# Moving the operands of the matrix products to other offsets within 128 bytes of on-chip memory

## The chip, the core and the metric

The kernel runs on one core of one Trainium2 chip. The metric is the device time of one execution in microseconds. The core has a matrix engine (TensorE; PE in the profile, its loads of stationary operands are PEld), three elementwise engines (VectorE = DVE, ScalarE = ACT, GpSimd = POOL), a queue engine (SyncE = SP) and 16 DMA engines. On-chip memory has 128 partitions; a tile has the same byte address in each of them, and this document speaks of that address: its remainder by 128 is called the offset here, offsets 0 to 63 are the low half and 64 to 127 the high half.

A product on PE has two operands in on-chip memory: a stationary block of 128 columns, which PEld loads into the array first, and moving rows (here 256, 260 or 512 columns), which stream through it. PEld loads the block of the next product while the moving rows of the present one stream.

## The reference

```
# q, k, v: 4 batches, 8 heads, 768 positions, 64 wide; n_sink = 4, window = 128
scores = q @ k^T / 8; kept where key < n_sink or 0 <= query - key < window, else -1e9
a = exp(scores - max); a = a / (sum(a) + 1e-9)
x = (a @ v), heads side by side: 3072 tokens x 512
h = x @ w_in            # 512 x 2048
g = h - tanh(h)
out = g @ w_out         # 2048 x 512, float32
```

## The kernel before

The 3072 tokens are cut into 12 chunks of 256, the 2048 hidden columns into 8 groups of 256. A step is one chunk with one group, 96 steps in all. Attention of a chunk is done for 4 pairs of heads (48 units); raw units work in float32, from the fourth chunk on queries and keys are split into a rounded high part and a rest (type float32r) and multiplied in pieces.

The first half of a step is 24 products of 256 columns (`mm1`, L793): a block of w_in is stationary, x is moving. x lies split in tiles xh (high) and xl (low). The blocks of w_in of the first three chunks (576 products) stand in resident tiles named w; for the later nine chunks (1728 products) they are streamed from DRAM into a ring of seven places, four in a tile named ring, three in one named spare, which hold 990 and 738 products.

The second half multiplies g with w_out. g lies split in tiles ghbuf and glbuf, whose blocks are stationary; w_out (tile w, or tile edge for derived sums of blocks) is moving. Steps of the first five chunks, and the last step, do it as 12 products of 512 columns (`mm2`, L863): 41 steps, 492 products. The other 55 steps use a scheme of seven block products, 21 products of 256 columns each (`mm7`, L897): 1155 products. The split scores (`scores`, L514) are 8 products of 260 columns for each of 36 units: 288, with a tile q as stationary and a tile ks as moving operand. Values times probabilities (L662), raw scores (L507) and transposes (L599, L640) are float32.

The order on each engine is written out by a planner (`Work.order`) from hand-given durations and due times; it knows nothing of addresses. Addresses come from the pools: tiles are laid one behind another in the order in which their pools and tags are opened, each start rounded up to 32 bytes. So a tile that is made longer moves all that lies behind it.

Of the kernel before, what the change touches and what calls it, by code (L numbers as in the profile page):

```python
# [9 lines left out]
F32 = mybir.dt.float32  # L10
F32R = mybir.dt.float32r
I32 = mybir.dt.int32
# [6 lines left out]
P = 128  # L19
# [7 lines left out]
KW = WIN + TS  # L27
KPACK = P + NT * TS
CH = 2 * P
# [10 lines left out]
@with_exitstack  # L40
def kernel(
    ctx: ExitStack,
    tc: tile.TileContext,
    qd: bass.AP,
    kp: bass.AP,
    vp: bass.AP,
    vs: bass.AP,
    nsw: bass.AP,
    w_in: bass.AP,
    w_out: bass.AP,  # L50
    xd: bass.AP,
    out: bass.AP,
):
    nc = tc.nc

    cpool = ctx.enter_context(tc.tile_pool(name="cpool", bufs=1))
    ident = cpool.tile([P, P], F32, tag="ident", name="ident")
    nswi = cpool.tile([P, 4], I32, tag="nswi", name="nswi")

    pts = cpool.tile([P, NPAIR, 2, 4, P], F32, tag="pt", name="pt")  # L60
    early = []
    for m in range(2):
        first = pts[:, m].rearrange("p h a b -> p (h a b)")
        early.append((first[:, :KW], first[:, KW : KW + 2 * CH].rearrange("p (h s) -> p h s", h=2)))
    et = mybir.EngineType
    with tc.manual_schedule(engines={et.PE, et.SP, et.DVE, et.Activation, et.Pool}):

        scr = pts[:, 2, 0]
        nc.sync.dma_start(nswi, nsw.partition_broadcast(P))
        for m in range(2):  # L70
            k, q = early[m]
            nc.sync.dma_start(k, kp[0, m, :, :KW])
            _load_pair(nc, q, qd[0, 2 * m : 2 * m + 2, :, :CH], True)
            if m == 0:
                make_identity(nc, ident)
                nc.gpsimd.iota(scr[:, 0, :].bitcast(I32), pattern=[[-1, P]], base=0, channel_multiplier=1)
                nc.gpsimd.iota(scr[:, 1, :].bitcast(I32), pattern=[[1, P]], base=0, channel_multiplier=0)
        masks = _masks(nc, cpool, nswi, scr)
        _, (nlo, nhi, wlo, whi) = nc.values_load_multi_w_load_instructions(
            nsw[0:1, 0:4], skip_runtime_bounds_check_because="every value takes one of the two branches"  # L80
        )
        bad = nhi | whi | ((nlo + 3) >> 3) | ((wlo - 1) >> 7)


        WARM = 3
        with tc.tile_pool(name="warm", bufs=1, space=PSUM) as wp:
            warm = wp.tile([P, P], F32, tag="warm", name="warm")
            for _ in range(WARM):
                nc.tensor.matmul(warm, lhsT=ident, rhs=ident, start=True, stop=True)

    with tc.If(bad == 0) as cmp:
        _banded(tc, qd, kp, vp, vs, masks, w_in, w_out, ident, pts, early, out)
    with cmp.Else():
        _general(tc, qd, kp, vp, nswi, w_in, w_out, ident, xd, out)


def _load_pair(nc, q, src, zeros):


    for h in range(2):  # L100
        r, z = slice(64 * h, 64 * h + 64), slice(64 * (1 - h), 64 * (1 - h) + 64)
        if zeros:
            nc.gpsimd.memset(q[z, h, :], 0.0)
        nc.sync.dma_start(q[r, h, :], src[h, r])
# [128 lines left out]
def _banded(tc, qd, kp, vp, vs, masks, w_in, w_out, ident, pts, early, out):  # L233
    nc = tc.nc
    et = mybir.EngineType
    with ExitStack() as ctx:

        def pool(name, bufs, **kw):
            return ctx.enter_context(tc.tile_pool(name=name, bufs=bufs, **kw))

        cpool, wpool, wmpool = pool("cpool", 1), pool("wpool", 1), pool("wmpool", 1)
        qpool, kpool, vpool, hpool = pool("qpool", 1), pool("kpool", 1), pool("vpool", 3), pool("hpool", 1)
        pp, sm = pool("pp", 2), pool("sm", 4)
        xpool, gpool = pool("xpool", 2), pool("gpool", 1)
# [8 lines left out]
        flat = wide.rearrange("p a b c -> p (a b c)")  # L253
        gbuf = gpool.tile([P, 8, P], F32, tag="gbuf", name="gbuf")
        ghbuf = gpool.tile([P, 2, 7, P], F32R, tag="ghbuf", name="ghbuf")
        glbuf = gpool.tile([P, 8, P], F32R, tag="glbuf", name="glbuf")
        wscr = dpool.tile([NG, P, 2 * WG], F32, tag="wscr", name="wscr")
        bscr = dpool.tile([NG, P, 5, DM // 2], F32, tag="bscr", name="bscr")
        kscr = dpool.tile([2, P, 2, DM // 2], F32, tag="kscr", name="kscr")
# [31 lines left out]
        qt, kt, vt, wraw = {}, {}, {}, {}  # L291
# [12 lines left out]
        def unit(u):  # L304
            cc, p = divmod(u, NPAIR)
            return (cc, p, *chunks[cc])
# [5 lines left out]
        def wtag(k, g):  # L312
            return f"w{k}_{g if k else g % NSLOT}"
# [5 lines left out]
        def load_qk(u):  # L319
            cc, p, b, c = unit(u)  # L320

            def lend():
                if u == 3:
                    if u not in place_of:
                        place_of[u] = gpool.tile([P, 3 * WG // 2], F32, tag="spare", name="qk3")
                    return place_of[u]
                if lent[u] not in place_of:
                    k, g = lent[u]
                    place_of[lent[u]] = wpool.tile([P, 2 * WG], F32, tag=wtag(k, g), name=f"qk{u}")
                return place_of[lent[u]][:, u % 2 * WG : u % 2 * WG + WG]  # L330

            def keys():
                if u in lent or u == 3:
                    kt[u] = lend()[:, 2 * CH : 2 * CH + KW]
                else:
                    kt[u] = kpool.tile([P, KW], F32, tag="kraw", name=f"kraw{u}")
                (nc.gpsimd if LQ and not raw(u) else nc.sync).dma_start(kt[u], kp[b, p, :, 2 * c * TS : 2 * c * TS + KW])

            def queries():
                if not raw(u):  # L340
                    qt[u] = qpool.tile([P, 2, CH], F32, tag="qraw", name=f"qraw{u}")
                src = qd[b, 2 * p : 2 * p + 2, :, c * CH : (c + 1) * CH]
                if raw(u):
                    _load_pair(nc, qt[u], src, False)
                else:
                    (nc.gpsimd if LQ else nc.sync).dma_start(qt[u], src.rearrange("h d s -> d h s"))  # L346

            def zeros():
                if u in lent or u == 3:
                    qt[u] = lend()[:, : 2 * CH].rearrange("p (h s) -> p h s", h=2)  # L350
                else:
                    qt[u] = qpool.tile([P, 2, CH], F32, tag="qraw", name=f"qraw{u}")
                nc.gpsimd.memset(qt[u], 0.0)

            t = due_unit(u) - 8000
            if raw(u):
                work.add("POOL", 460, t - ZL, zeros, (), [slots(u)[1]])
            e = "POOL" if LQ and not raw(u) else "SP"
            work.add(e, 600, t, keys, (), [slots(u)[0], "seq k"], lands=800 if raw(u) else 1000)
            work.add(e, 800, t, queries, (), [slots(u)[1], "seq q"], lands=600 if raw(u) else 1000)  # L360

# [49 lines left out]

        zt = cpool.tile([P, 2, NPAIR, 4, 2, NSK], F32R, tag="z", name="z")

        zr = cpool.tile([P, 2, CH], F32R, tag="zr", name="zr")

        mask, above, below, after, rest = masks

# [44 lines left out]
        qh, ql, ks, pr, st, xps, xh, xl, sps, tps = ({} for _ in range(10))  # L462

        def split(u):

            def k_high(h):
                if h == 0:
                    t = hpool.tile([P, NPAIR * CH], F32R, tag="ha", name=f"ks{u}")  # L470
                    ks[u] = t[:, : 2 * KW].rearrange("p (h k) -> p h k", h=2)
                r = slice(64 * h, 64 * h + 64)
                nc.scalar.copy(ks[u][r, h, :], kt[u][r, :])  # L473

            def k_low(h):
                k, t = ks[u], kt[u]
                r, o = slice(64 * h, 64 * h + 64), slice(64 * (1 - h), 64 * (1 - h) + 64)
                (nc.gpsimd if KP else nc.vector).tensor_tensor(k[o, h, :], t[r, :], k[r, h, :].bitcast(F32), op=ALU.subtract)  # L478

            def q_high():  # L480
                t = hpool.tile([P, 2, 2, CH], F32R, tag="hb", name=f"q{u}")
                qh[u], ql[u] = t[:, 0], t[:, 1]
                nc.scalar.copy(qh[u], qt[u])

            def q_low():
                (nc.gpsimd if QP else nc.vector).tensor_tensor(ql[u], qt[u], qh[u].bitcast(F32), op=ALU.subtract)  # L486

            t = due_unit(u) - 5000
            k, q = ([s] for s in slots(u))
            old = [("x", 2)] + [("xu", 2, i) for i in range(NPAIR)] if u == 3 * NPAIR else []  # L490
            work.add("ACT", 525, t, q_high, q, ["qh"] + old)
            work.add("POOL" if QP else "DVE", 1360 if QP else 705, t, q_low, q + ["qh"], ["ql"], port=True)
            for h in range(2):
                work.add("ACT", 425, t, lambda h=h: k_high(h), k, [("ks", h)] + old)
                work.add("POOL" if KP else "DVE", 1050 if KP else 590, t, lambda h=h: k_low(h), k, [("ks", h)], port=True)
# [853 lines left out]
```

## Time and profile before

| | before |
|---|---|
| median of 3 runs | 687.06 us (685.87 to 687.35) |
| the profiled execution: its time | 685.92 us |
| its span, first to last instruction | 684.2 us |
| granted TensorE clock, mean of the span | 0.997 |
| PE busy | 665.0 us, 97% |
| DVE / ACT / POOL busy | 78% / 60% / 30% |

The profiled execution is 1.14 us below the median. Its time is 1.7 us longer than its span. PE's record of a product lasts from its start to the modelled end of the pipeline, so records overlap: what a product costs in a stream is the distance from its start to the start of the next.

### The profile page before, as it was taken

Reading aid. Unit: us, or ns where it says so; the run is one execution under the profiler, and the core shown is the slowest. Engines: PE = TensorE matmul, PEld = TensorE weight load, DVE = VectorE, ACT = ScalarE, POOL = GpSimd, SP = SyncE. Lnnn points to the kernel's source line nnn. Section 1 sums busy time; section 2 is a strip of 40 time slices with the busy share of each in tenths; the row PEclk is TensorE's granted clock in tenths of the full one; section 3 lists DMA queues with packets and bytes.
Section 4 is the critical chain, followed back from the end, with each engine's and each line's share of the span. In section 5 each row is a group of like instructions: output and inputs, shape, how many; then the busy total and the mean of one; then the engine's idle time right before and its main releaser. Section 6 shows DMA issues by size and latency. Waiting matters only on the chain.

```text
span 684.2 us, 14570 instructions
## 1 busy us (share of the span) xinstructions
PE 665.0 (97%) x5099; PEld 613.8 (90%) x5099; DVE 531.4 (78%) x1365; ACT 412.7 (60%) x1056; POOL 204.7 (30%) x363
## 2 busy tenths in 40 slices
PE   6899999999999999999999999999999999999995
PEld 4677899989888898899999999999999999999995
DVE  6999988965998875577698797888888888755654
ACT  5986444435998876466676576676676567533331
POOL 5444000002985532334432323422223222300100
PEclk9999999999999999999999999999999999999998
DMA  6878896785999577799977767766667766656861
GB/s 178 269 252 273 283 308 242 285 280 155 199 209 289 182 228 222 216 290 284 265 223 215 230 176 233 231 209 207 215 216 231 245 192 168 206 160 196 261 187 35
DMA packets 79342, 152.96 MB, mean 224 GB/s; under 512 B 9565, under 2 KB 25565, under 8 KB 79261
## 3 DMA queue, kind: packets, MB, share of 16 engines
q1 hardware_dynamic: 65884, 121.65, 56.7%
q0 software_dynamic: 13376, 30.30, 16.4%
q8 instruction: 42, 0.69, 0.4%
q14 instruction: 40, 0.32, 0.1%
HBM read 131.47 MB, written 20.45 MB: 222 GB/s over the span
## 4 chain that ended last, share of the span: by engine, by line
PE 83%; POOL 4%; DVE 4%; ACT 4%; DMA 2%; issue 2%; SPq 0%; POOLq 0%; DVEq 0%; ACTq 0%
PE h L793 35%; PE s L897 11%; PE o L897 8%; PE o L863 8%; PE x L662 3%; PE s L863 3%; PE t L599 2%; PE t L662 2%; PE t L514 2%; PE t L863 2%; PE x L514 2%; PE x L863 2%; POOL edge L995 1%; PE s L514 1%; DMA v<-vp 1%
## 5 line engine op out<-in xcount | busy, mean ns | idle before, releaser
L793 PE MATMUL h<-xh,ring 128*128 128x256 f32 x660 | 133.5, 282 | 0.0
L812 ACT ACTIVATE gbuf<-h 128x512 f32<-128x512 f32 x96 | 57.2, 596 | 86.7 <-PE h L793 58.9
L793 PEld LDWEIGHTS h<-xh,ring 128*128 128x128 f32 x660 | 107.8, 188 | 0.4 <-PE t L662 0.2
L793 PE MATMUL h<-xh,spare 128*128 128x256 f32 x492 | 100.0, 283 | 0.0
L346 POOL DMA_DIRECT2D qraw<-qd x36 | 29.6, 821 | 222.7 <-DVE q L486 198.4
L793 PE MATMUL h<-xl,ring 128*128 128x256 f32 x330 | 92.2, 279 | 0.0
L539 ACT ACTIVATE p<-p,st 128x132 f32<-128x132 f32 x168 | 66.9, 400 | 27.8 <-DVE st L531 26.6
L831 ACT CAST ghbuf<-gbuf 128x896 fp32r<-128x896 f32 x55 | 51.8, 942 | 49.0 <-DVE gbuf L828 48.6
L793 PEld LDWEIGHTS h<-xh,spare 128*128 128x128 f32 x492 | 81.0, 190 | 0.3
L834 DVE TENSOR_TENSOR glbuf<-gbuf,ghbuf 128x896 fp32r<-128x896 f32 x55 | 60.3, 1097 | 20.1 <-ACT ghbuf L831 15.1
L793 PE MATMUL h<-xh,w 128*128 128x256 f32 x384 | 74.0, 282 | 0.0
L793 PE MATMUL h<-xl,spare 128*128 128x256 f32 x246 | 69.4, 282 | 0.0
L793 PEld LDWEIGHTS h<-xl,ring 128*128 128x128 f32 x330 | 62.1, 188 | 0.3
L793 PEld LDWEIGHTS h<-xh,w 128*128 128x128 f32 x384 | 61.1, 188 | 1.3 <-PE x L662 0.2
L565 ACT ACTIVATE p<-p,st 128x132 f32<-128x132 f32 x168 | 54.2, 394 | 3.5 <-DVE st L560 3.1
L815 DVE TENSOR_TENSOR gbuf<-h,gbuf 128x512 f32<-128x512 f32 x55 | 37.8, 687 | 21.9 <-ACT gbuf L812 21.3
L793 PE MATMUL h<-xl,w 128*128 128x256 f32 x192 | 53.8, 280 | 0.0
L619 POOL TENSOR_TENSOR pt<-pt,after 128x512 f32<-128x512 f32 x32 | 44.1, 1379 | 25.5 <-ACT pt L616 24.1
L863 PE MATMUL o<-w,ghbuf 128*128 128x512 f32 x192 | 50.8, 399 | 0.1
L793 PEld LDWEIGHTS h<-xl,spare 128*128 128x128 f32 x246 | 46.7, 190 | 0.3
L815 DVE TENSOR_TENSOR h<-h,gbuf 128x512 f32<-128x512 f32 x41 | 28.5, 695 | 19.1 <-ACT gbuf L812 19.0
L478 DVE TENSOR_TENSOR ks<-kraw,ks 64x392 fp32r<-64x392 f32 x72 | 40.5, 562 | 3.5 <-ACT ks L473 1.4
(174 smaller groups left out, 1693.2 us busy)
## 6 DMA issues: line engine op xcount, KB each, us to landing
ring<-wscr SPq DMA_DIRECT2D x165, 256.0 KB, 4.3
spare<-wscr SPq DMA_DIRECT2D x123, 256.0 KB, 4.5
qraw<-qd POOLq DMA_DIRECT2D x36, 256.0 KB, 5.2
wraw<-w_in SPq DMA_DIRECT2D x16, 512.0 KB, 6.4
wraw<-w_out SPq DMA_DIRECT2D x16, 512.0 KB, 6.9
wscr<-w SPq DMA_DIRECT2D x16, 512.0 KB, 6.0
kraw<-kp POOLq DMA_DIRECT2D x36, 196.0 KB, 4.5
v<-vp POOLq DMA_DIRECT2D x18, 256.0 KB, 3.3
```

The lines of the kernel that those rows point to most:

```text
L478: (nc.gpsimd if KP else nc.vector).tensor_tensor(k[o, h, :], t[r, :], k[r, h, :].bitcast(F32), op=ALU.subtract)
L514: nc.tensor.matmul(ps[h][:, :WIN], lhsT=q[:, h, t * P : (t + 1) * P], rhs=rhs, start=i == 0, stop=i == 1,)
L539: nc.scalar.activation(e, e, AF.Exp, bias=st[u][:, j : j + 1], scale=-1.0, accum_out=st[u][:, 4 + j : 5 + j],)
L565: nc.scalar.activation(pr[u][:, j, :], pr[u][:, j, :], AF.Copy, scale=s[:, 8 + j : 9 + j])
L619: nc.gpsimd.tensor_tensor(w[:, :, 0, :], w[:, :, 0, :], after.unsqueeze(1).to_broadcast([P, 4, P]), op=ALU.mult)
L793: nc.tensor.matmul(hps[n][:, f, :], lhsT=w, rhs=x, start=r == 0, stop=r == 11)
L812: nc.scalar.activation(g0, h(), AF.Tanh)
L815: nc.vector.tensor_tensor(g0 if strassen(n) else h(), h(), g0, op=ALU.subtract)
L831: nc.scalar.copy(ghbuf[:, n % 2], gbuf[:, 1:, :])
L834: nc.vector.tensor_tensor(glbuf[:, :7, :], gbuf[:, 1:, :], ghbuf[:, n % 2].bitcast(F32), op=ALU.subtract)
L863: nc.tensor.matmul(sums_of(n, cc, t), lhsT=a[:, f, t * P : (t + 1) * P], rhs=wt[1, g][:, (0, 1, 0)[i], f, :], start=first and not low and ...
L897: nc.tensor.matmul(acc, lhsT=a[:, b, :], rhs=factor(g, m, part % 2), start=g == 0 and part == 0 and m in (4, 1, 2, 7), stop=closes(n) and ...
```

## The change

Five tiles are made longer or start later, and the views used by the program are cut out of them, so no instruction is added, taken away or reordered: on all five engines the program has the same rows in the same order. What is different are the addresses of operands.

```
-    nswi = cpool.tile([P, 4], I32, tag="nswi", name="nswi")
+    nswi = cpool.tile([P, 12], I32, tag="nswi", name="nswi")[:, :4]
...
-        glbuf = gpool.tile([P, 8, P], F32R, tag="glbuf", name="glbuf")
+        glbuf = gpool.tile([P, 8 * P + 16], F32R, tag="glbuf", name="glbuf")[:, : 8 * P].rearrange("p (b t) -> p b t", b=8)
...
-                    kt[u] = kpool.tile([P, KW], F32, tag="kraw", name=f"kraw{u}")
+                    kt[u] = kpool.tile([P, KW + 8], F32, tag="kraw", name=f"kraw{u}")[:, :KW]
...
-        zr = cpool.tile([P, 2, CH], F32R, tag="zr", name="zr")
+        zr = cpool.tile([P, 2 * CH + 24], F32R, tag="zr", name="zr")[:, : 2 * CH].rearrange("p (r c) -> p r c", r=2)
...
-                    ks[u] = t[:, : 2 * KW].rearrange("p (h k) -> p h k", h=2)
+                    ks[u] = t[:, 16 : 16 + 2 * (KW + 24)].rearrange("p (h k) -> p h k", h=2)[:, :, :KW]
```

The offsets (address modulo 128) in the two built programs; blocks and rows of one tile are multiples of 512 bytes apart, so that all of them have the tile's offset, but for ks:

| operand | before | after |
|---|---|---|
| xh, xl (moving, L793) | 96 | 0 |
| ring, w (stationary, L793) | 64 | 64 |
| spare (stationary, L793) | 96 | 64 |
| w, edge (moving, L863, L897) | 64 | 64 |
| ghbuf, glbuf (stationary, L863, L897) | 96 | 0 |
| ks (moving, L514): first head, second head | 96 or 112; 0 or 16 | 64 or 80; 64 or 80 |
| q (stationary, L514) | 96 | 0 |

Taken by pairs, the moving rows of one product and the block that PEld loads meanwhile: before, the two lie in the same half in nearly all pairs of L793, L863 and L897, and in half of the pairs of L514. They lie 32 bytes apart at L793 with ring and w, 0 bytes apart with spare, and 32 bytes the other way at L863 and L897. After, they lie 64 bytes apart (64 or 80 at L514), in different halves. The pairs at a change from one line to another are the exception: after, 277 of the 4238 pairs of these four lines still share a half. Modulo 256 the third chunk stands alone before: its 192 products of L793 have their moving rows at 224, all other chunks at 96, against w and ring at 64 and spare at 96.

## Rows read from the trace of the kernel before

**Rows 1.** The page's part 1: engine, busy us, share of span, instructions.
```profile
PE 665.0 (97%) x5099; PEld 613.8 (90%) x5099; DVE 531.4 (78%) x1365; ACT 412.7 (60%) x1056; POOL 204.7 (30%) x363
```

**Rows 2.** Four stretches: us, busy us by engine (instructions), clock, DMA share, GB/s.
```profile
0.00:60.00 60.00, 50.53 (x303) 38.40 (x303) 49.26 (x207) 46.96 (x173) 29.59 (x77) 1.00 0.76 239
60.00:204.00 144.00, 142.05 (x939) 125.93 (x938) 119.78 (x219) 80.86 (x185) 39.22 (x57) 1.00 0.82 247
204.00:640.00 436.00, 435.24 (x3563) 413.48 (x3563) 339.14 (x901) 273.81 (x685) 134.75 (x229) 1.00 0.73 221
```

**Rows 3.** Waits, the longest of ACT: who waited for whom, us, times, longest.
```profile
ACT gbuf L812 <- PE h L793: 58.9, 28, 4.4
```

**Rows 4.** Timeline of PE, blocks from spare: start us, us, line, count.
```profile
405.87 0.28 PE L793 MATMUL h<-xh,spare 128*128 128x256 f32 x1
405.98 0.28 PE L793 MATMUL h<-xl,spare 128*128 128x256 f32 x1
...
407.90 0.28 PE L793 MATMUL h<-xh,spare 128*128 128x256 f32 x1
408.01 0.28 PE L793 MATMUL h<-xh,ring 128*128 128x256 f32 x1
```

**Rows 5.** Timeline of PE, blocks from ring: eighteen products between these starts.
```profile
364.66 0.28 PE L793 MATMUL h<-xh,ring 128*128 128x256 f32 x1
...
366.76 0.28 PE L793 MATMUL h<-xh,spare 128*128 128x256 f32 x1
```

**Rows 6.** Timeline of PE, resident w: 12 products at L863, 24 at L793, alternating.
```profile
100.86 2.02 PE L863 MATMUL s<-w,ghbuf 128*128 128x512 f32 x8
...
103.65 0.28 PE L793 MATMUL h<-xh,w 128*128 128x256 f32 x1
...
106.46 1.09 PE L863 MATMUL t<-w,ghbuf 128*128 128x512 f32 x4
...
109.25 0.28 PE L793 MATMUL h<-xh,w 128*128 128x256 f32 x1
...
112.09 2.02 PE L863 MATMUL s<-w,ghbuf 128*128 128x512 f32 x8
```

**Rows 7.** Timeline of PE, twice 21 products at L897 and the start after them.
```profile
602.39 0.64 PE L897 MATMUL s<-edge,ghbuf 128*128 128x256 f32 x4
...
604.88 0.28 PE L793 MATMUL h<-xh,spare 128*128 128x256 f32 x1
...
645.62 0.64 PE L897 MATMUL s<-edge,ghbuf 128*128 128x256 f32 x4
...
648.10 0.28 PE L793 MATMUL h<-xh,ring 128*128 128x256 f32 x1
```

**Rows 8.** Timeline of PE, float32 products: four records at each of two lines.
```profile
25.42 1.04 PE L507 MATMUL s<-qk 128*128 128x260 f32 x4
26.30 0.60 PE L599 MATMUL t<-ident,wide 128*128 128x128 f32 x4
26.74 0.38 PE L640 MATMUL x<-ident,z 128*128 128x128 f32 x2
```

**Rows 9.** Timeline of PE, split scores: two products of each head, then the next line.
```profile
479.70 0.40 PE L514 MATMUL t<-ks,q 128*128 128x260 f32 x2
479.94 0.40 PE L514 MATMUL x<-ks,q 128*128 128x260 f32 x2
480.18 0.28 PE L793 MATMUL h<-xh,ring 128*128 128x256 f32 x1
```

**Rows 10.** One line's instructions at L793: duration ns min/median/max, first and last start.
```profile
L793 PEld LDWEIGHTS h<-xh,ring x660: 186/188/193, 204.1 to 671.3; 128*128 128x128 f32 x165
L793 PEld LDWEIGHTS h<-xh,spare x492: 187/189/232, 208.1 to 670.6; 128*128 128x128 f32 x164
```

## The prediction, made before the run

> **What bounds the kernel now.** First the shares of busy time: PE is busy for 665.0 of 684.2 us, DVE for 78% of the span, ACT for 60% [rows 1]. Then the same by stretches, to see where PE is really the bound: from 60 us to 640 us PE is busy for 577.3 of 580 us, while DVE has 24 us free in the second stretch and 97 us in the third [rows 2]. Only the first 60 us, with 9.5 us of PE idle, wait for others. Third the waits: the longest of an arithmetic engine is ACT waiting 58.9 us for products of L793 [rows 3]. So PE sets the end, and others wait for it. PE runs 4502 of its 5099 products in these two stretches [rows 1, 2], so there a nanosecond off a product is taken as a nanosecond off the time.
>
> Fourth the timeline of PE, for the distance from start to start, with the granted clock at 1.00 (the 2.4 GHz level) in these stretches [rows 2]. Products of the same shape on the same line do not cost the same:
>
> - blocks from spare (0 bytes apart): 18 products from 405.87 to 408.01, 118.9 ns each, of which 16 steps from 405.98 to 407.90 are 120.0 each [rows 4]. I take 119.0.
> - blocks from ring (32 bytes apart): 18 products in 2.10 us, 116.7 ns [rows 5].
> - resident w: 24 products in 2.81 us, 117.1 ns, for one chunk, and in 2.84 us, 118.3 ns, for the next, the third one, whose moving rows lie at another offset modulo 256 [rows 6].
> - L897 (32 bytes the other way): 21 products in 2.49 and in 2.48 us, 118.6 and 118.1 ns [rows 7]. I take 118.3.
> - L863, the same tiles and offsets as L897, 512 columns: 12 products in 2.79 us, 232.5 ns [rows 6].
> - L514: 4 products of 260 columns in 0.48 us, 120 ns [rows 9].
>
> The loads of blocks from spare have a median of 189 ns, those from ring of 188 [rows 10]. All that differs between ring and spare is the address. So the address does matter to PE, by 2.3 ns of 117.
>
> **The change part by part.** It adds no instruction and no wait, so the longer tiles themselves cost nothing on any engine. What it can change is the distance between products. Two parts of that distance can be separated.
>
> The part that the load of the next block can be to blame for: L897 and L863 have the same offsets, and two products of 256 columns stream as many columns as one of 512. 2 x 118.3 - 232.5 = 4.1 ns is what one more product costs beyond its columns, a load collision and a fixed start cost together. For the fixed cost the float32 rows serve: four records of 260 columns take 0.88 us, four of 128 take 0.44 us [rows 8], 220 and 110 ns, a slope of 110/132 = 0.833 ns a column and a rest of 110 - 106.7 = 3.3 ns. Whether that holds for float32r is not shown, so the collision at L897 and L863 is between 4.1 - 3.3 = 0.8 and 4.1 ns. Elsewhere it follows from the difference to 118.3: spare 1.5 to 4.8, third chunk 0.8 to 4.1, L514 (120 less 4 columns at 0.45 is 118.2) 0.7 to 4.0, other resident w 0 to 2.9, ring 0 to 2.5.
>
> If different halves take the collision away, the saving is, in us:
>
> - low end: 738 x 1.5 + (1155 + 492 + 192) x 0.8 + 288 x 0.7 = 1.1 + 1.5 + 0.2 = 2.8
> - high end: 738 x 4.8 + (1155 + 492 + 192) x 4.1 + 288 x 4.0 + 990 x 2.5 + 384 x 2.9 = 3.5 + 7.5 + 1.2 + 2.5 + 1.1 = 15.8
> - a value between, if every pair comes to the best rate in these rows, ring's 116.7: 738 x 2.3 + (1155 + 492 + 192) x 1.6 + 288 x 1.5 + 384 x 0.4 = 1.7 + 2.9 + 0.4 + 0.2 = 5.2
>
> I take 6.0: near the measured 5.2, since that asks for no rate that is not in the trace, with a little for pairs 64 bytes apart being better than 32. Continuing the step from 0 to 32 bytes once more (another 2.3) would lead to the high end, which is why it stays in the range.
>
> The rest of the distance, some 0.45 ns a column at 512 columns against the 0.417 that half of the float32 slope would be, grows with the moving columns and not with the loads; I leave it as it is.
>
> The Trainium skill speaks against any gain: "TensorE: Matmul & The Clock Gate", Part 2, step 1, has two independent read ports in PE, so that loading the next block takes nothing from the running product, and "SBUF — State Buffer", section "Who interferes with whom", has PE wait for nobody. By that rule the sum would be 0. The trace does not agree in full: two equal streams differ by 2.3 ns with the address alone [rows 4, 5].
>
> The elementwise engines and DMAs read and write the moved tiles too. What their instructions gain or lose by it no row shows; the cover is DVE's free 121 us between 60 and 640 us [rows 2], and a 1% longer DVE would use about 5 of them. I put it at 0.
>
> The profiled execution took 685.92 us; less 6.0 that is 679.9. It is 1.14 us under the median, so against the median of 687.06 the forecast is **681.0 us**.
>
> **The rivals.**
>
> *Nothing happens*: 687.1 us. For it: at L514 two of four products have operands in the same half and two in different ones (ks of the first head at 96 or 112, of the second at 0 or 16, q at 96), and the pairs start 0.24 us apart in either case [rows 9]. Against it: such pairs are short, and the 120.0 of spare shows only in a long row [rows 4]; ring, spare and the third chunk differ steadily.
>
> *The whole excess is a collision of the two streams*: then 256 columns cost 0.417 x 256 = 106.7 plus a start of 2 to 3 ns, about 109, and 512 about 216. Saved: 738 x 10 + 990 x 7.7 + 384 x 8.1 + (1155 + 192) x 9.3 + 492 x 16.5 + 288 x 8 = 7.4 + 7.6 + 3.1 + 12.5 + 8.1 + 2.3 = 41 us, 646 us; with half of it 666.5 us. For it: the excess exists and nothing in the clock explains it. Against it: L863's 232.5 ns has one load for 512 columns and twice the excess, which a collision with one load doesn't give. I price this case at 666.5.
>
> The skill's gap for back-to-back products, N/2.4 + 2.5 ns ("TensorE: Matmul & The Clock Gate", section "Back-to-back issue gap"), would give 109.2 and 215.8 ns, the same end; no row of a float32r product here reaches it.
>
> *Slower*: the two streams 64 bytes apart fall into the beat that spare shows, 120.0 ns with longer loads, because what decides is not the half but the distance modulo a smaller unit; the place is the rows of L793 from ring, which are the fastest now. Price if all pairs went there: 738 x 1.0 + 990 x 3.3 + 384 x 2.9 + (1155 + 492 + 192) x 1.7 + 288 x 1.8 = 0.7 + 3.3 + 1.1 + 3.1 + 0.5 = 8.7 us, 695.8 us. It decides once ring's distance rises above about 119. For it: 32 bytes one way and the other give 116.7 and 118.3, so distance alone is no good order. Against it: it would have to hit nearly all lines.
>
> That the change doesn't do what it says can be left out: the offsets stand in the built program, and 3961 of 4238 pairs lie in different halves.
>
> **How the numbers follow.** Chances: small gain 0.42 (own range 671 to 684.3, from 15.8 and 2.8), nothing 0.27, whole or half excess 0.18, slower 0.13. About 0.2% or 1.4 us is what a measurement can tell from no change here. Faster is the first and third case less a little, 0.59; the same 0.28; slower 0.13. The range reaches from 664, just past half of the whole excess, to 689, a quarter of the slower case; left out are about 0.09 below and 0.09 above.
>
> **What would show it.** Right: in the timeline of the changed kernel, spare and ring cost the same, at about 116, L897 about 116.5, L863 about 231, and the loads from spare take 188 ns. Nothing: 117, 119 and 118.3 as before. The whole excess: 109 to 113 at L793 and under 225 at L863, and then ACT and DVE wait less for PE. Wrong in sign: rows of 120 with ring. The forecast is also wrong if PE gets faster but its idle time between 60 and 640 us, 2.7 us now, grows by as much, with waits for DVE in its place.

## The result, and the profile after

The changed kernel takes 680.9 us (median of 4 runs, 680.65 to 681.68) where the kernel before takes 686.46 us (4 runs, 685.36 to 687.35) beside it. The ratio is 0.992, 95% interval 0.9901 to 0.9939: 5.5 us less, between 4.2 and 6.8. The profiled execution took 680.82 us, its span is 679.0 us; before, 685.92 and 684.2.

The page's first part and the two long stretches (columns as in [rows 1, 2]), and ACT's longest wait [rows 3], of the changed kernel:

```profile
PE 659.7 (97%) x5099; PEld 608.8 (90%) x5099; DVE 531.6 (78%) x1365; ACT 412.7 (61%) x1056; POOL 204.3 (30%) x363
```

```profile
60.00:204.00 144.00, 142.20 (x944) 126.08 (x943) 120.40 (x219) 81.06 (x186) 39.16 (x58) 1.00 0.82 248
204.00:640.00 436.00, 434.89 (x3602) 413.10 (x3601) 342.34 (x906) 275.02 (x685) 135.55 (x229) 1.00 0.73 223
```

```profile
ACT gbuf L812 <- PE h L793: 57.7, 29, 4.4
```

PE is as full as before: it idles for 2.9 us between 60 and 640 us (2.7 before), at the same granted clock, while 44 more of its products begin there (4546 for 4502). DVE's busy time has not moved (531.6 for 531.4 us). So the time came out of the distance between products, and no other engine took it back.

The timeline of PE around one step of resident w, answering to [rows 6]: 12 products at L863, 24 at L793, 12 at L863, 24 at L793 of the third chunk.

```profile
101.04 2.02 PE L863 MATMUL s<-w,ghbuf 128*128 128x512 f32 x8
...
103.83 0.28 PE L793 MATMUL h<-xh,w 128*128 128x256 f32 x1
...
106.66 1.10 PE L863 MATMUL t<-w,ghbuf 128*128 128x512 f32 x4
...
109.46 0.28 PE L793 MATMUL h<-xh,w 128*128 128x256 f32 x1
...
112.19 1.55 PE L863 MATMUL s<-w,ghbuf 128*128 128x512 f32 x6
```

L863 costs 2.79 us for 12 again, 232.5 ns. The 24 of the second chunk cost 2.83 us, 117.9 ns (117.1 before); those of the third 2.73 us, 113.8 ns (118.3 before).

Then ring, spare and L897, answering to [rows 4, 5, 7], in three stretches of the same timeline:

```profile
363.14 0.28 PE L793 MATMUL h<-xh,ring 128*128 128x256 f32 x1
...
365.18 0.28 PE L793 MATMUL h<-xh,spare 128*128 128x256 f32 x1
...
366.54 0.64 PE L897 MATMUL s<-edge,ghbuf 128*128 128x256 f32 x4
...
600.61 0.28 PE L793 MATMUL h<-xh,spare 128*128 128x256 f32 x1
...
602.03 0.28 PE L793 MATMUL h<-xh,ring 128*128 128x256 f32 x1
...
603.44 0.63 PE L897 MATMUL s<-edge,ghbuf 128*128 128x256 f32 x4
...
605.83 0.28 PE L793 MATMUL h<-xh,ring 128*128 128x256 f32 x1
...
640.88 0.63 PE L897 MATMUL s<-edge,ghbuf 128*128 128x256 f32 x4
...
643.35 0.28 PE L793 MATMUL h<-xh,ring 128*128 128x256 f32 x1
```

18 products from ring take 2.04 us and 12 from spare 1.36 us in the first, 113.3 ns both. In the second the same pairings take 118.3 (spare) and 117.5 (ring), and 21 products of L897 take 2.39 us, 113.8 ns. In the third L897 takes 2.47 us, 117.6 ns. One and the same line with the same addresses modulo 256 runs in two beats (steady distances from start to start), near 113.4 and near 117.8 ns, and changes between them from stretch to stretch.

The loads, answering to [rows 10] (ns, minimum, median, maximum):

```profile
L793 PEld LDWEIGHTS h<-xh,ring x660: 186/188/192, 203.8 to 666.1; 128*128 128x128 f32 x165
L793 PEld LDWEIGHTS h<-xh,spare x492: 187/188/194, 207.9 to 665.4; 128*128 128x128 f32 x164
```

Because of the two beats a single row says little. The table has the mean over the steps from start to start within a row (products of one line and tile that nothing interrupts), without the row's first step, worked out from all records of both traces. The distance is the address of the moving rows less that of the block loaded meanwhile, modulo 256: the experiments below show that this orders the results better than the half does.

| products | distance before, after | ns before, after | us saved |
|---|---|---|---|
| L897, 1155 | 224, 192 | 118.3, 115.6 | 3.1 |
| spare, 738 | 0, 192 | 119.1, 115.7 | 2.5 |
| third chunk, 192 | 160, 192 | 118.5, 114.6 | 0.75 |
| ring, 990 | 32, 64 | 117.1, 116.7 | 0.4 |
| L514, 288 | mixed | 120.0, 119.4 | 0.2 |
| other resident w, 384 | 32, 64 | 116.9, 117.8 | -0.35 |
| L863, 492 | 224, 192 | 232.8, 233.2 | -0.2 |

The sum is 6.4 us; the spans differ by 5.2. The table multiplies by all products, also those before a change of line or a wait, where the gain is not seen: added up over the steps inside rows alone, its lines without L514 give 5.6 us. And the changed kernel begins L793 0.4 us later (42.33 us for 41.93).

Counted by rows of at least six products, the fast beat (a mean under 115.5 ns) has 29 of 60 rows of L897, 21 of 65 of spare, 6 of 8 of the third chunk, and also 27 of 82 of ring, whose distance is 64. The kernel before has no such row.

### The profile page after: what moved, and what is told of

Same layout as the page of the kernel before. It is cut to its first block, busy times and chain, and to the rows that moved or that the text cites. A ratio compares the mean times of both kernels' runs of the same rounds, so it can differ in the third digit from the quotient of the medians.

```text
span 679.0 us, 14570 instructions
## 1 busy us (share of the span) xinstructions
PE 659.7 (97%) x5099; PEld 608.8 (90%) x5099; DVE 531.6 (78%) x1365; ACT 412.7 (61%) x1056; POOL 204.3 (30%) x363
## 4 chain that ended last, share of the span: by engine, by line
PE 74%; ACT 6%; DVE 5%; POOL 5%; issue 4%; DMA 4%; POOLq 0%; DVEq 0%; ACTq 0%
PE h L793 31%; PE s L897 10%; PE o L897 7%; PE o L863 6%; PE s L863 3%; PE x L662 3%; PE t L599 2%; PE t L662 2%; PE t L863 2%; PE t L514 2%; PE x L863 2%; PE x L514 1%; ACT p L565 1%; DMA w<-bscr 1%; POOL edge L995 1%
## 5 line engine op out<-in xcount | busy, mean ns | idle before, releaser
L793 PE MATMUL h<-xh,ring 128*128 128x256 f32 x660 | 133.2, 281 | 0.0
L793 PEld LDWEIGHTS h<-xh,ring 128*128 128x128 f32 x660 | 107.6, 188 | 0.6 <-issue 0.2
L793 PE MATMUL h<-xh,spare 128*128 128x256 f32 x492 | 97.7, 280 | 0.0
L793 PE MATMUL h<-xl,ring 128*128 128x256 f32 x330 | 91.9, 278 | 0.0
L793 PEld LDWEIGHTS h<-xh,spare 128*128 128x128 f32 x492 | 80.0, 188 | 0.3
L793 PE MATMUL h<-xh,w 128*128 128x256 f32 x384 | 73.7, 281 | 0.0
L793 PE MATMUL h<-xl,spare 128*128 128x256 f32 x246 | 68.6, 279 | 0.0
L793 PEld LDWEIGHTS h<-xl,ring 128*128 128x128 f32 x330 | 62.0, 188 | 0.3
L793 PEld LDWEIGHTS h<-xh,w 128*128 128x128 f32 x384 | 60.9, 188 | 1.3 <-PE x L662 0.2
L793 PE MATMUL h<-xl,w 128*128 128x256 f32 x192 | 53.6, 279 | 0.0
L863 PE MATMUL o<-w,ghbuf 128*128 128x512 f32 x192 | 50.9, 399 | 0.1
L793 PEld LDWEIGHTS h<-xl,spare 128*128 128x128 f32 x246 | 46.4, 188 | 0.2
```

Source lines behind the costliest of these rows:

```text
L793: nc.tensor.matmul(hps[n][:, f, :], lhsT=w, rhs=x, start=r == 0, stop=r == 11)
L863: nc.tensor.matmul(sums_of(n, cc, t), lhsT=a[:, f, t * P : (t + 1) * P], rhs=wt[1, g][:, (0, 1, 0)[i], f, :], start=first and not low and ...
```

## The experiments

Theory A is the prediction's: the halves of 128 bytes decide. Theory B came from the rows above: the distance modulo 256 decides, in some form of its own. D, later, adds that the block's own place on a grid of 32 bytes counts. The programs of one session ran beside the kernel before; every ratio is against it. The experiments on the whole kernel have the same instructions and waits as the changed kernel; only addresses differ.

**Products alone.** Rows of 36 products with nothing else running, one row for each distance:

```
+ def row(far, cols, n, shift=0):          # far: bytes between block and moving rows
+     o, s = (far + shift) // 4, shift // 4
+     for i in range(n):
+         nc.tensor.matmul((a, b)[i % 2][:, :cols], lhsT=block[:, s + i % 4 * P : s + i % 4 * P + P],
+                          rhs=moving[:, o : o + cols], start=True, stop=True)
```

> A program of TensorE products alone: the reference's computation is left out, only some rows of one product are written. Rows of 36 float32r products of 256 columns, four stationary blocks in turn, the moving rows starting 0, 16, ... 496 bytes after the block modulo 512 (twice, in two orders), then distances 0, 64, 128, 192 with both operands shifted by 0 to 224 bytes, then rows of 18 products of 512 columns at 16 distances. Theory A (halves of 128 bytes): start to start is lowest for every pair that lies in different halves, the same at 64, 192, 320 and 448, some 115 ns against 117 to 120 at 0 and 128. Theory B (distance modulo 256, one-sided): about 113.4 to 115.6 around 192 and 448, 117 to 118 at 64 and 320, 119 to 120 at 0, no matter where the pair as a whole lies. Both: 512 columns stay at 232 to 234 at every distance.

Three of its rows in the timeline of PE; L65 is the row's first product, L60 the small float32 products behind it; the distances are 64, 112 and 192:

```profile
27.16 0.36 PE L65 MATMUL pa<-moving,block 128*128 128x256 f32 x1
...
31.48 0.60 PE L60 MATMUL pc<-ident 128*128 128x128 f32 x4
...
41.31 0.36 PE L65 MATMUL pa<-moving,block 128*128 128x256 f32 x1
...
45.52 0.60 PE L60 MATMUL pc<-ident 128*128 128x128 f32 x4
...
64.73 0.36 PE L65 MATMUL pa<-moving,block 128*128 128x256 f32 x1
...
68.92 0.60 PE L60 MATMUL pc<-ident 128*128 128x128 f32 x4
```

A row of 36 takes 4.32, 4.21 and 4.19 us. Its first product costs some 85 ns more than the others and the next few are uneven; from the seventh on the means are 117.8, 114.2 and 113.3 ns. At 112 even that mean is not the steady beat: the first eight to fourteen products are uneven, near 118, and those behind them take 113.3 as at 192. Means from the seventh product on:

| distance | 0 | 32 | 64 | 96 | 112 | 128 | 160 | 192 | 224 |
|---|---|---|---|---|---|---|---|---|---|
| ns, 256 columns | 120.0 | 116.7 | 117.8 | 120.0 | 114.2 to 114.9 | 118.7 | 117.3 to 118.7 | 113.3 or 117.8 | 118.3 |

256 to 496 bytes repeat 0 to 240. Block and rows shifted together in steps of 32 give the same as unshifted, but for 192, which takes 113.3 in five of these eight rows and 117.8 in three. With 512 columns distances 0 and 64 give 228.8 ns, all others 231 to 236.7 (192: 233.3), where both theories had expected 232 to 234 everywhere. That refutes A: at 96 the operands lie in different halves, and the row is as slow as at 0; at 32 they lie in the same half, and it is faster; 64 and 192 both lie in different halves, and of the two only 192 shows the fast beat in this run. The unit is 256. With nothing else running on the core the same two beats show at 192, so neither DMAs nor the elementwise engines are needed for them.

**The blocks of g alone.** On the kernel before, ghbuf and glbuf are moved to distance 192 from their moving rows; L793 stays as it was.

```
-        gbuf = gpool.tile([P, 8, P], F32, tag="gbuf", name="gbuf")
+        gbuf = gpool.tile([P, 8 * P + 8], F32, ...)[:, : 8 * P]
-        glbuf = gpool.tile([P, 8, P], F32R, tag="glbuf", name="glbuf")
+        glbuf = gpool.tile([P, 8 * P + 56], F32R, ...)[:, : 8 * P]
```

> The kernel before, with only the g blocks (ghbuf and glbuf) moved by 32 bytes, so that L897 and L863 have the distance they have in the changed kernel; all other pairs as before. Theories A and B alike: L897 falls from 118.3 to 115.6 ns, 1155 x 2.7 = 3.1 us, L863 stays at 233, L793 stays (119.1 spare, 117.1 ring), so about 683.4 us. Rival C (the gain comes from where xh and xl lie, or from the elementwise engines that write them): L897 stays at 118.3, 686.5 us.

Measured: 685.07 us, ratio 0.9973 (0.9957 to 0.9988), 1.9 us less. L897 falls to 115.8 ns as in the changed kernel, L863 stays at 233.0, spare at 119.4, ring at 117.3. So the place of the g blocks alone does it, and rival C is refuted; the lines that were not moved stay within 0.8 ns. Of L897's 2.5 ns x 1155 = 2.9 us, 1.9 arrive: inside rows it gains 2.4 us, and ring and spare, 0.3 ns slower, lose 0.4.

**The other half, on the other side.** From the changed kernel, all pairs to distance 64, where A sees no difference:

```
-                    kt[u] = kpool.tile([P, KW + 8], F32, ...)
+                    kt[u] = kpool.tile([P, KW + 40], F32, ...)
-                    st[u] = sm.tile([P, 12], F32, ...)
+                    st[u] = sm.tile([P, 20], F32, ...)[:, :12]
-        gbuf = gpool.tile([P, 8, P], F32, ...)
+        gbuf = gpool.tile([P, 8 * P + 32], F32, ...)[:, : 8 * P]
```

> The changed kernel with spare, the third chunk's xh and xl and the g blocks moved on by 128 bytes, so that every pair still lies in different halves of 128 bytes, but all at distance 64 modulo 256 and none at 192. Theory A: nothing changes, 680.9 us. Theory B: spare from 115.8 to 117.0 (738 x 1.2 = 0.9 us), L897 from 115.6 to 117 or 118 (1155 x 1.4 to 2.2 = 1.6 to 2.5 us), third chunk from 114.6 to 117.8 (0.6 us), 684 to 685 us.

```profile
602.16 0.63 PE L897 MATMUL s<-edge,ghbuf 128*128 128x256 f32 x4
...
604.63 0.28 PE L793 MATMUL h<-xh,spare 128*128 128x256 f32 x1
```

```profile
101.90 2.01 PE L863 MATMUL s<-w,ghbuf 128*128 128x512 f32 x8
103.74 0.62 PE L863 MATMUL s<-w,glbuf 128*128 128x512 f32 x2
```

684.42 us, 0.9953 (0.9939 to 0.9967). L897 is back at 2.47 us for 21, 117.6 ns; means of the lines at L793 and L897 lie between 117.3 and 117.7, and the fast beat is down to 1 of 60 rows of L897 and 15 of 148 of ring and spare. A, by which nothing changes, is refuted by these rows; the time says it less surely, since its interval overlaps that of the second measurement of the changed kernel below (0.9911 to 0.9954). B's 684 to 685 is met. What nobody expected: L863 drops, 8 products in 1.84 us, 229.9 ns in the mean. 512 columns want another distance than 256, and those 492 x 2.9 = 1.4 us are half of what this kernel still gains on the one before.

**All pairs to 192.** From the changed kernel, ring and resident w too:

```
+                    st[u] = sm.tile([P, 20], F32, ...)[:, :12]
+        gbuf = gpool.tile([P, 8 * P + 32], F32, ...)[:, : 8 * P]
-        glbuf = gpool.tile([P, 8 * P + 16], F32R, ...)[:, : 8 * P]
+        glbuf = gpool.tile([P, 8 * P + 48], F32R, ...)[:, : 8 * P]
```

> The changed kernel with xh and xl (but those of the third chunk) and spare moved on by 128 bytes, so that all pairs of L793, L863 and L897 lie at distance 192 modulo 256. Theory A: nothing changes, 680.9 us. Theory B: ring from 116.7 to 115.5 (990 x 1.2 = 1.2 us), resident w of two chunks from 117.8 to 114.2 (384 x 3.6 = 1.4 us), spare as it is, 678.3 us.

```profile
601.38 0.29 PE L793 MATMUL h<-xh,spare 128*128 128x256 f32 x1
...
604.12 0.63 PE L897 MATMUL s<-edge,ghbuf 128*128 128x256 f32 x4
```

681.71 us, 0.9925 (0.991 to 0.994), no better than the changed kernel where B said 678.3. The 24 products here run at 2.74 us, 114.2 ns, and the means of ring (115.4) and w (114.6) fell as B said; but L897 rose to 116.8 and the third chunk to 117.25, at addresses that had not moved against each other. So more than a line's own distance decides which beat it gets; the next run asks whether what ran before does.

**What turns the beat.** Products alone again: other distances, and the same four with 1 to 8 small products between the rows.

> Products alone again, the reference's computation left out. Rows of 36 products of 256 columns at distances 8, 24, ... 248 and 100, 108, 116, 124, twice; then 32, 64, 112 and 192, each after gaps of one to eight small products; then 260 columns and 512 columns at 16 distances. If the distance modulo 256 alone sets the beat (theory B): 32 near 116.7, 64 at 117.8 and 112 at 114 to 115 after every gap, 192 at 113.3 or 117.8 depending on the gap; the distances between two steps of 16 lie near their neighbours; 512 columns at 228.8 for 0 and 64 and 231 to 236 elsewhere. If the history sets it as much as the distance (theory C): 32, 64 and 112 scatter over the gaps by 2 ns or more too.

Two rows at distance 192, behind one and behind two small products (each leaves two records at L60):

```profile
216.43 0.36 PE L65 MATMUL pa<-moving,block 128*128 128x256 f32 x1
...
220.76 0.60 PE L60 MATMUL pc<-ident 128*128 128x128 f32 x4
...
235.03 0.37 PE L65 MATMUL pa<-moving,block 128*128 128x256 f32 x1
...
239.21 0.83 PE L60 MATMUL pc<-ident 128*128 128x128 f32 x6
```

4.33 and 4.18 us: 117.8 and 113.3 ns. Of eight gaps the odd ones gave 117.8, the even ones 113.3. That is no rule: in the last run below, at 192 on the grid, all four rows behind three small products were fast, and three of four behind two were slow. Distance 112 gave 114.2 to 114.4 (113.3 in the steady part) and distance 64 gave 117.8 behind every gap; 32 gave 117.8 behind one small product and 116.5 to 116.9 behind the others. So the history can move 32 too, by 1.2 ns, which is more than B and less than C expected. Distances off a grid of 16 bytes gave mostly 120 (104 bytes: 130.0), 260 columns 118.3 to 121.9 at any distance, 512 columns 226.7 at 0, 228.9 at 64, 231.1 at 112 and 233.3 at 192.

**All 256-column pairs to 112**, the distance that was fast behind every gap:

```
+        gall = gpool.tile([P, 22 * P + 28], F32R, ...)[:, 4 : 22 * P + 4]      # ghbuf and glbuf cut from it
+        xall = xpool.tile([P, 4 * NPAIR * CH + 12], F32R, ...)[:, 12:]         # xh and xl of two homes cut from it
```

> The changed kernel with xh and xl, and the g blocks, moved so that L793 (but for the third chunk), L897 and L863 have distance 112 modulo 256; same instructions, same waits. Of these, L793 has its operands in different halves of 128 bytes and L897 and L863 have them in the same half. Theory B (distance modulo 256): 114.5 ns at L793 and L897, 231 at L863; against before 990 x 2.6 + 738 x 4.6 + 384 x 2.4 + 192 x 2.5 + 1155 x 3.8 + 492 x 1.7 = 12.6 us less, of which some 0.85 arrives as it did for the changed kernel, so about 676 us where before takes 687. Theory A (halves of 128 bytes): L897 back to 118.3, so 684 to 685.

```profile
601.92 0.65 PE L902 MATMUL s<-edge,gall 128*128 128x256 f32 x4
...
604.44 1.58 PE L798 MATMUL h<-xall,spare 128*128 128x256 f32 x12
605.86 1.53 PE L798 MATMUL h<-xall,ring 128*128 128x256 f32 x12
607.23 0.65 PE L902 MATMUL s<-edge,gall 128*128 128x256 f32 x4
```

685.55 us, 0.9985 (0.9967 to 1.0003): no difference that this tells. L902, which is L897 here, takes 2.52 us for 21, 120.0 ns, instead of 114.5; L793 lies at 116.2. B failed: the distance is not enough. For L902 one difference is at hand: the blocks of gall start 16 bytes off the 32-byte grid, and in the programs of products alone so far all blocks lay on it.

L793's blocks lie on the grid, and its 116.2 has another cause, which the lines above show: the first 12 products of this stretch take 1.42 us, 118.3 ns each, the next 12 take 1.37 us, 114.2. Over all stretches of L793 the means of the first eleven steps lie between 116.4 and 118.9 ns, those from the twelfth on near 113.4. That is the slow beginning which 112 has alone too; here a stretch has between 5 and 30 products, and two thirds of the steps fall into it.

**The same, with L863 at 64.**

```
+            return ghbuf[:, r]...[:, 12 : 2 * CH + 12], gall[:, 14 * P + 12 + r * 2 * CH : ...]
```

> As the one at 112, but the g blocks of the 512-column products start 48 bytes later, so that L863 has distance 64. Theory B: L863 at 229 to 230.3 instead of 231 to 233, 492 x 2 = 1 us less, about 675 us where before takes 687; L793 and L897 at 114.5. Theory A: L863 unchanged at 233, the same time as the one at 112.

684.31 us, 0.9959 (0.9942 to 0.9976). L863 falls from 232.65 to 229.5 ns, 492 x 3.2 = 1.6 us, as B said; the third chunk, untouched, goes from 116.2 to 114.6. B's 675 us is missed, since L793 and L902 stay where they were.

**All pairs to 0**, with 96 the worst distance of the first run for 256 columns and among the best for 512:

```
-        xall = xpool.tile([P, 4 * NPAIR * CH + 12], ...)[:, 12:]
+        xall = xpool.tile([P, 4 * NPAIR * CH + 48], ...)[:, 48:]
-        gall = gpool.tile([P, 22 * P + 28], ...)[:, 4 : 22 * P + 4]
+        gall = gpool.tile([P, 22 * P], ...)
```

> The changed kernel with all pairs of L793 (but the third chunk), L897 and L863 at distance 0. Theory B: 120 ns at L793 and L897, 229 at L863; against before 990 x 2.9 + 384 x 3.1 + 738 x 0.9 + 1155 x 1.7 - 492 x 3.8 - 192 x 1.5 = 4.5 us more, 691 to 692 us where before takes 687. Theory A: both operands in the same half as before, 687.

```profile
101.64 2.88 PE L868 MATMUL s<-w,gall 128*128 128x512 f32 x12
...
104.36 0.52 PE L798 MATMUL h<-xall,w 128*128 128x256 f32 x3
```

690.0 us, 1.0046 (1.0028 to 1.0063): addresses alone can make this kernel slower too. All lines of 256 columns run at 119.7 to 119.8, only the third chunk at 117.2, and L863 (L868 here) at 2.72 us for 12; its mean is 228.8. B's 691 to 692 for 687, a ratio of 1.006 to 1.007, was near; A's 1.000 lies outside.

**The changed kernel again, and L863 at 0.** Three kernels side by side: the changed kernel as it is; with L863's blocks 192 bytes on, so that its distance is 0; and the same on the kernel with all pairs at 192.

```
+            return ghbuf[:, r]...[:, 48 : 2 * CH + 48], gflat[:, 48 + r * 2 * CH : 48 + (r + 1) * 2 * CH]
```

> The changed kernel once more, beside the next two on one chip: 0.992 of the time of before, as it was.

> The changed kernel with the g blocks of the 512-column products 192 bytes further in their tiles, so that L863 has distance 0 instead of 192; all other pairs as in the changed kernel. Theory B (measured distances): L863 from 233.2 to 228.8 ns, 492 x 4.4 = 2.2 us, of which 1.8 to 2.2 arrive: 0.989 of before, some 2 us under the changed kernel. Theory A (different halves are better): L863 loses instead, or stays at 233, so no gain over the changed kernel.

> The kernel with all pairs at 192, with L863 at 0 as well: by the same step 2 us under that kernel's 0.9925, so 0.9895; L793 near 115 and L897 near 117 as they were there.

```profile
101.58 1.98 PE L864 MATMUL s<-w,ghbuf 128*128 128x512 f32 x8
103.39 0.84 PE L864 MATMUL s<-w,glbuf 128*128 128x512 f32 x3
```

The changed kernel: 682.01 us, 0.9933 (0.9911 to 0.9954). L863 at 0: 680.65 us, 0.9918 (0.9896 to 0.9941). Both: 681.21 us, 0.9916 (0.9896 to 0.9936). L863 (L864 here) falls as expected, 8 in 1.81 us above, 229.0 in the mean (233.2), which is worth 2.1 us; but the third chunk turns to 117.3 and takes back 0.5. In the third kernel resident w, with the addresses that it had in the kernel with all pairs at 192, goes back from 114.6 to 117.1, 384 x 2.5 = 1.0 us. The intervals overlap: that either beats the changed kernel is not shown.

**The block off the grid.** Products alone, block and rows shifted together in steps of 16 bytes:

```
+        for gap in (2, 3):
+            for shift in range(0, 128, 16):
+                for far in (0, 32, 64, 112, 128, 192):
+                    row(far, 256, 36, shift)
+                    warm(gap)
```

> Products alone, the reference's computation left out: rows of 36 products of 256 columns at distances 0, 32, 64, 112, 128, 192, with both operands shifted by 0, 16, ... 112 bytes, after gaps of two and of three small products. If the distance alone counts, each distance has one value for all shifts (192 its two), and 112 stays at 114.2. If an operand off the 32-byte grid costs as well (theory D, from L897 at 119.7 with its blocks at 80 and its moving rows at 192), then distance 112 is 114.2 with the block on the grid and the moving rows off it (shifts 0, 32, 64, 96) and about 119.7 with the block off it (shifts 16, 48, 80, 112), and the even distances rise at odd shifts too.

Distance 112 with the block at 0, and with the block at 16; then distance 64 with the block at 96:

```profile
22.27 0.37 PE L65 MATMUL pa<-moving,block 128*128 128x256 f32 x1
...
23.66 0.28 PE L65 MATMUL pb<-moving,block 128*128 128x256 f32 x1
...
26.50 0.60 PE L60 MATMUL pc<-ident 128*128 128x128 f32 x4
...
50.24 0.37 PE L65 MATMUL pa<-moving,block 128*128 128x256 f32 x1
...
54.59 0.60 PE L60 MATMUL pc<-ident 128*128 128x128 f32 x4
...
186.19 0.36 PE L65 MATMUL pa<-moving,block 128*128 128x256 f32 x1
...
190.36 0.49 PE L60 MATMUL pc<-ident 128*128 128x128 f32 x3
```

4.23 and 4.35 us; from the seventh product on 114.4 and 118.4 ns. The first of these rows takes 1.39 us for 11 products, 118.6 ns each without the 85 of its start, and 2.84 us for the other 25, 113.6 ns. On the grid 112 gives 113.9 to 114.8, off it 118.4 at three shifts and 120.0 at the fourth, where the block lies at 80 modulo 128; the blocks of gall lie there too, and L902's 119.8 agrees. So D holds for 112. It does not hold as a general price: off the grid distance 0 falls from 119.9 to between 116.6 and 118.4, and 192 gives 113.3 to 114.0 in all eight rows, where on the grid five of eight are fast. The third row shown is at 64 and on the grid: 4.17 us, 113.3 ns from the seventh product on. It and one row off the grid are the only fast ones of 16 at that distance (the others: 117.8 on the grid, 118.3 off it), so the fast beat is rare at 64, but not absent. A kernel with all pairs at 192 and the blocks off the grid was not tried.

## Why the prediction was right, and where not

**PE sets the end, and a nanosecond off a product is one off the time**: held. Idle 2.7 and 2.9 us, ACT's wait for L793 1.2 us shorter, no new wait in place of the gain. But it holds for products inside a row (5.6 us by their steps, 5.2 by the spans); taken times all products it is too much (6.4).

**The size, 6.0 us**: held; 5.5 (4.2 to 6.8) was measured, and the working value of 5.2, every pair at 116.7, is nearest. But that the sum came out was luck: its terms compensated. L897 and spare brought more than priced (1155 x 1.6 = 1.8 and 1.7; measured 3.1 and 2.5), the third chunk 0.75 for 0.3. L863 was to give 492 x 1.6 = 0.8 and gave -0.2; resident w 384 x 0.4 = 0.2 and gave -0.35.

**"Different halves take the collision away"**: the step that failed. Halves of 128 do not order the rows (alone 96, in different halves, takes 120.0 and 32, in the same half, 116.7); the distance modulo 256 orders them better, with the block's place on the 32-byte grid and with what ran before. The gain of this change is that L897, spare and the third chunk came to 192 and spend about half of their time in the beat of 113.4: a mean of 115.6 is midway between 113.4 and 117.8. With the same pairs in different halves at 64 the means are 117.3 to 117.7 and the time 684.42 us. "64 bytes being better than 32" was no sure gain either: alone 117.8 in 27 rows of 28 on the grid, against 116.7; in the changed kernel resident w lost 0.9 ns by it, and ring won 0.4, by the rows in the fast beat. And the collision of a load with the moving rows is not shown as such: the runs show a time that follows the addresses of the two, not what in PE makes it.

**The separation of a cost per load by 2 x 118.3 - 232.5**: the form was wrong. If each load had a price of its own that the distance sets, twice the 256-column time less the 512-column time would be positive at every distance. Alone it is 2 x 120.0 - 228.8 = 11.2 ns at 0, and at 192 in the fast beat 2 x 113.3 - 233.3 = -6.7 ns. The two widths prefer different distances (0 is among the slowest for 256 columns and the fastest for 512), and this is why L863 did not follow L897. Of the signs that the prediction named, L863 at about 231 is the one that failed outright; ring and spare came to within 1 ns of each other, and the loads from spare take 188 ns.

**Nothing happens** (0.27): refuted by the interval. The Trainium skill's two independent read ports ("TensorE: Matmul & The Clock Gate", Part 2, step 1), by which a load takes nothing from the running product, leave no room for this. The rows do not agree: 113.3 against 120.0 ns by addresses alone, with nothing else running; the measurement decides. **The whole excess**: alone no row of 256 columns fell under 113.3 or of 512 under 226.7, so its 109 and 216 are not there by any address tried. The Trainium skill's N/2.4 + 2.5 ns ("TensorE: Matmul & The Clock Gate", section "Back-to-back issue gap", which gives it for an isolated product), an estimate of 109.2 and 215.8 ns here, is not reached by these float32r products. **Slower**, by all lines in the beat of 120: not here, but it is a real place. Its price was 8.7 us over the median; with the pairs of L793 (but the third chunk), L897 and L863 at 0 the kernel was 3.2 us slower, in part because L863 gained 2.0 us there.

Elementwise engines at 0: held (DVE busy 531.4 and 531.6 us).

**Open**: why one distance has two beats (192 often, 64 now and then), and what chooses between them; why 112 needs eight to fourteen products to come to its beat; why a block off the 32-byte grid loses at 112 and gains at 0 and 192; and whether the block that counts is the one loaded meanwhile or the product's own, which in the rows of products alone have the same offset.

## What to carry to other kernels

When PE is full and two rows of the same shape differ by a few nanoseconds, look at the addresses of the moving rows and of the block loaded meanwhile before looking at waits: here they moved the whole kernel between 0.992 and 1.005 without one instruction changed. Measure a curve of products alone for the width in use, since 256 and 512 columns want different distances. Look at its first products as well as at its steady part, since rows in a kernel are short: 112 lost most of its gain there. Then measure the kernel. Let means over all steps of a line decide, not one row: where a line has two beats, any one row shows whichever beat it is in.

## What was not expected of the hardware

- The time of a float32r product of 256 columns goes in steps with the distance of its operands modulo 256 bytes: 113.3, 116.7, 117.8, 118.7, 120.0 ns, and 130.0 at 104 bytes.
- One distance can have two beats: alone and on the 32-byte grid, 192 took 113.3 ns in 16 rows of 28 and 117.8 in 12, and 64 took 113.3 in 1 of 28. In one run an even number of small products before the row gave the fast beat at 192 and an odd one the slow; in another three gave the fast one each time.
- At distance 112 the steady beat of 113.3 ns comes only after eight to fourteen products near 118, in products alone as in the kernel.
- 512 columns: 226.7 to 228.8 ns at 0, 233.3 at 192, 236.7 at 240; 260 columns have no good distance (118.3 to 121.9 ns).
